# Attention in 32-column tiles, score groups of three PSUM banks, separate rings for weight pieces

## The chip, the cores and the metric

The kernel runs on one core of one Trainium2 chip. A core has a matrix engine (TensorE, PE in the profile, with its weight loads in a row of their own, PEld), a vector engine (DVE), a scalar engine (ACT), GpSimd (POOL, which here only starts DMAs) and a sync engine (SP, which only starts DMAs). Each engine works through its own list of instructions in order and waits on semaphores. The metric is the time of one execution on the device in microseconds (us); less is better.

## The reference

Attention with capped scores over 4 batches and 12 heads, 448 positions, head size 64, and then two layers that are alike: `relu(x @ w_in) ** 2 @ w_out`, for 1792 tokens, with 768 and 2048 columns.

```python
scores = scale * np.matmul(q, k.transpose(0, 1, 3, 2))
scores = cap * np.tanh(scores / cap)
scores = scores - np.max(scores, axis=-1, keepdims=True)
attn = np.exp(scores)
attn = attn / (np.sum(attn, axis=-1, keepdims=True) + 1e-09)
x = np.matmul(attn, v)            # then (tokens, 768)
h = np.maximum(x @ w_in, 0.0)
x = h * h @ w_out                 # and once more with other weights
```

The weights come as float64. The kernel takes their two words as integers and makes float32 of them.

## The kernel before

**Attention** goes over 24 pairs of heads, A and B, one pair a step (`PAIRS`). The keys of a pair make seven tiles of 128: three of A, three of B, and one tile R with the last 64 keys of both heads. Scores stand transposed, keys on partitions and the 448 queries along the row, so each score matmul is 128x448 in float32, which the trace shows as two MATMULs. In step n PE does, in this order (`attention`, the loop at the end): the scores of pair n, where A's matmul uses rows 0 to 63 of the array and B's rows 64 to 127, both at once (L321); the totals of pair n-1, a sum over keys by a matmul with 32 columns of ones, four at once into the four quarters of bank 7 (L367); the values of pair n-1, two matmuls of 64 columns at once into the halves of bank 6 (L353); the scores of tile R of pair n, over all 128 rows and columns (L321); the values of tile R of pair n-1, likewise (L349). ACT takes tanh in place and then exp out of PSUM (L334, L338), by groups of two tiles (`GROUPS`), with R alone; the groups of a pair take turns on three places of two banks each (ring `sc`: banks 0, 2, 4). DVE transposes the totals out of bank 7, adds quarters in four instructions, takes the reciprocal, transposes back (L376 to L388) and multiplies the values in bank 6 by it (L406).

**The layers** do each product in seven block products (a Strassen scheme, `NAMES`), each as three matmuls of split operands: high part of the weight by high and low part of x, low part of the weight by high part of x (L658 to L660), 4032 matmuls of 128x128 by 128x448 in all. Weights come in 224 pieces of six 128x128 blocks. A piece is loaded from DRAM by SP (`load` in `run_pass`, L623), ACT rounds its high part into a buffer `wh` (L591, 3 buffers), and DVE takes the difference (L186) into `wl`: before, that is the buffer in which the piece was loaded, so one ring of 6 buffers `wl` holds a piece from its load to PE's last use of it.

**Rounding of words.** `round_words` turns 68 units of float64 words into float32: SP loads a unit (`ww`, 2 buffers, L206), ACT scales the high words (L212), DVE does three bit operations (L215, L218, L221), POOL stores it. Each two units make a block, of which DVE also makes four sums (L244) that POOL stores; the buffers `wg` (4) are free after that. A unit must be stored before the weight pieces that read it are loaded.

**The order** of each engine's list comes from a planner (`Plan`): every operation has an engine, a cost, a place on a common scale (one unit is one weight piece, 18 matmuls; attention lies before 0, a step is `STEP` units), a due time that sorts the engine's candidates, and rings that it takes from and gives back to. The planner writes the lists; at run time each engine only follows its own. The due times of rounding come from a loop that spreads blocks over the scale by a rate (`room`, L749 to L757).

## Time and profile before

| what | us |
|---|---|
| median of 3 runs | 1054.51 (1054.08 to 1054.87) |
| the profiled execution: its own time | 1051.55 |
| the profiled execution: its span, first to last instruction | 1049.6 |
| PE busy | 1026.8 (98%) |
| DVE busy | 846.2 (81%) |
| ACT busy | 707.2 (67%) |
| PEld busy | 828.7 (79%) |
| POOL busy | 106.8 (10%) |

A busy share is a mean over the whole span. The program has two stages that differ: attention up to the first MATMUL of L658, and the layers. Rows of stretches (busy time in a stretch), of the chain that ended last, and of single instructions in order of time tell the stages apart.

### The profile page before, as it was taken

The page shows a single profiled execution, that of the slowest core. Times are in us where ns is not written, and L with a number is a line of the kernel's source. Part 1 is how long each engine was busy: PE and PEld are TensorE (multiplying, and loading weights), DVE is VectorE, ACT ScalarE, POOL GpSimd, SP SyncE. Part 2 cuts the span into 40 slices and gives each one's busy share as a digit, 9 for nine tenths or more (in the row PEclk, how much of TensorE's full clock was granted, in tenths as well). Part 3 has the DMA queues.
Part 4 walks back from the last instruction along what each step waited for, and adds up shares of the span by engine and source line. Part 5 has one row for each costly group of instructions (what it writes and reads, how often), then busy time and mean ns, then how long its engine had stood idle before and what let it go on. Part 6 is the DMA issues. An engine that isn't in the chain of part 4 may idle for free.

```text
span 1049.6 us, 15159 instructions
## 1 busy us (share of the span) xinstructions
PE 1026.8 (98%) x5088; PEld 828.7 (79%) x5088; DVE 846.2 (81%) x1252; ACT 707.2 (67%) x1011; POOL 106.8 (10%) x185
## 2 busy tenths in 40 slices
PE   7999999999999999999999999999999999999997
PEld 3333333499998899989898998898999999999996
DVE  3789887878899989888999999779996865589751
ACT  7999999777786664777865746778565444465641
POOL 0100121212111011011110121111000000000000
PEclk9999999999999999999999999999999999999999
DMA  8868899789878497679774976987556533334341
GB/s 208 277 208 253 266 288 329 256 292 294 278 240 278 136 330 249 224 264 317 253 236 138 341 264 197 299 287 249 175 153 218 157 112 107 105 111 124 113 146 53
DMA packets 106726, 231.53 MB, mean 221 GB/s; under 512 B 16336, under 2 KB 61648, under 8 KB 106640
## 3 DMA queue, kind: packets, MB, share of 16 engines
q1 hardware_dynamic: 91920, 171.88, 53.6%
q0 software_dynamic: 14720, 58.60, 14.6%
q8 instruction: 42, 0.69, 0.3%
q14 instruction: 44, 0.36, 0.1%
HBM read 166.33 MB, written 64.09 MB: 220 GB/s over the span
## 4 chain that ended last, share of the span: by engine, by line
PE 88%; DVE 5%; DMA 3%; issue 2%; ACT 1%; SPq 0%; POOL 0%; DVEq 0%; ACTq 0%; POOLq 0%
PE bank L660 23%; PE bank L659 23%; PE bank L658 23%; PE bank L321 8%; PE bank L353 6%; PE bank L367 4%; PE bank L349 2%; DMA ww<-wout_dram 2%; DVE wl L186 1%; DVE xc L186 1%; DVE wg L244 1%; DMA wl<-wo 1%; DVE wg L218 1%; DMA wo<-wg 1%; ACT p L338 0%
## 5 line engine op out<-in xcount | busy, mean ns | idle before, releaser
L660 PE MATMUL bank<-xc,wl 128*128 128x448 f32 x1344 | 492.8, 367 | 7.1 <-DVE wl L186 7.0
L658 PE MATMUL bank<-xc,wh 128*128 128x448 f32 x1344 | 492.4, 366 | 1.9 <-ACT xc L519 1.6
L659 PE MATMUL bank<-xc,wh 128*128 128x448 f32 x1344 | 492.1, 366 | 1.3 <-DVE xc L186 1.3
L591 ACT ACTIVATE wh<-wl 128x768 fp32r<-128x768 f32 x224 | 188.6, 843 | 198.9 <-PE bank L659 171.5
L186 DVE TENSOR_TENSOR wl<-wl,wh 128x768 fp32r<-128x768 f32 x224 | 211.5, 953 | 85.4 <-ACT wh L591 84.8
L660 PEld LDWEIGHTS bank<-xc,wl 128*128 128x128 f32 x1344 | 252.4, 188 | 32.0 <-DVE wl L186 10.4
L658 PEld LDWEIGHTS bank<-xc,wh 128*128 128x128 f32 x1344 | 252.5, 188 | 24.4 <-ACT xc L519 2.0
L659 PEld LDWEIGHTS bank<-xc,wh 128*128 128x128 f32 x1344 | 252.4, 188 | 23.8 <-DVE xc L186 1.9
L677 ACT ACTIVATE one<-bank 128x448 f32<-128x448 f32 x132 | 71.1, 539 | 66.5 <-PE bank L660 61.8
L321 PE MATMUL bank<-raw 64*128 64x448 f32 (+1 forms) x336 | 88.6, 575 | 6.2 <-DMA raw<-qk_dram 4.8
L334 ACT ACTIVATE bank<-bank,caps 128x896 f32<-128x896 f32 x96 | 84.5, 880 | 8.7 <-PE bank L321 8.4
L338 ACT ACTIVATE p<-bank,caps 128x896 f32<-128x896 f32 x96 | 87.8, 914 | 3.1
L679 DVE TENSOR_TENSOR one<-bank,one 128x448 f32<-128x448 f32 x96 | 59.0, 620 | 28.9 <-PE bank L660 22.2
L321 PEld LDWEIGHTS bank<-raw 64*128 64x128 f32 (+1 forms) x336 | 34.7, 191 | 57.6 <-ACT bank L334 16.5
L218 DVE SCALAR_TENSOR_TENSOR wg<-ww,wg 128x768 uint32<-128x768 uint32 (+1 forms) x68 | 61.9, 910 | 2.0
L221 DVE SCALAR_TENSOR_TENSOR wg<-ww,wg 128x768 uint32<-128x768 uint32 (+1 forms) x68 | 61.7, 907 | 1.6
L212 ACT ACTIVATE wg<-ww 128x768 f32<-128x768 f32 (+1 forms) x68 | 57.8, 860 | 5.8 <-DMA ww<-wout_dram 3.6
L353 PE MATMUL bank<-p,vr 128*64 128x448 f32 x288 | 59.4, 548 | 0.0
L353 PEld LDWEIGHTS bank<-p,vr 128*64 128x64 f32 x288 | 18.5, 136 | 39.8 <-issue 29.6
L186 DVE TENSOR_TENSOR xc<-ga,xc 128x896 fp32r<-128x896 f32 (+1 forms) x50 | 45.1, 916 | 0.7 <-ACT xc L519 0.6
L215 DVE TENSOR_SCALAR wg<-wg 128x768 uint32<-128x768 uint32 (+1 forms) x68 | 36.0, 530 | 9.0 <-ACT wg L212 9.0
L367 PE MATMUL bank<-p,ones 128*32 128x448 f32 x384 | 41.1, 545 | 0.0
(80 smaller groups left out, 828.4 us busy)
## 6 DMA issues: line engine op xcount, KB each, us to landing
ww<-win_dram SPq DMA_DIRECT2D x32, 768.0 KB, 6.8
wl<-si SPq DMA_DIRECT2D x120, 192.0 KB, 3.9
wl<-wi SPq DMA_DIRECT2D x96, 192.0 KB, 3.7
ww<-wout_dram SPq DMA_DIRECT2D x24, 768.0 KB, 7.5
wi<-wg POOLq DMA_DIRECT2D x32, 384.0 KB, 6.3
si<-wg POOLq DMA_DIRECT2D x32, 384.0 KB, 4.9
wl<-so SPq DMA_DIRECT2D x32, 384.0 KB, 3.8
raw<-qk_dram SPq DMA_DIRECT2D x48, 240.0 KB, 5.1
```

Of the source, the lines that this page charges most:

```text
L186: nc.vector.tensor_tensor(out, a, b, op=ALU.subtract)
L218: nc.vector.scalar_tensor_tensor(m["fu"], m["t"][:, :n, 0], 29, m["fu"], op0=ALU.logical_shift_right, op1=ALU.bitwise_or)
L321: nc.tensor.matmul(s["s"][:, i, :S], lhsT=stk["t"][rows, S + 128 * t:S + 128 * t + 128], rhs=stk["t"][rows, :S], start=True, stop=True)
L334: nc.scalar.activation(s["s"], s["s"], AF.Tanh, scale=rcap)
L338: nc.scalar.activation(s["p"], s["s"], AF.Exp, scale=capt)
L353: nc.tensor.matmul(bank[64 * e:64 * e + 64, 6, :S], lhsT=vt["t"][:, w:w + 64], rhs=s["p"][:, e], start=gi == 0, stop=False, skip_group_che ...
L367: nc.tensor.matmul(bank[32 * z:32 * z + 32, 7, :S], lhsT=ones[:, one], rhs=p, start=half == 0, stop=half == 1)
L591: nc.scalar.activation(m["hi"], m["f"], AF.Copy)
L658: nc.tensor.matmul(a, lhsT=hi, rhs=x(0), start=first and z == 0, stop=False, skip_group_check=more)
L659: nc.tensor.matmul(a, lhsT=hi, rhs=x(1), start=False, stop=False, skip_group_check=more)
L660: nc.tensor.matmul(a, lhsT=lo, rhs=x(0), start=False, stop=final and z == len(xs) - 1, skip_group_check=more)
L677: nc.scalar.activation(m[g, i, n], a, AF.Copy)
```

## The change

In attention everything on PE but the scores of the tiles of A and B now uses tiles of 128 rows and 32 columns, four at once: the values of the first three tile pairs (rows in `PARTS` order: A, B, A, B, each half of 32), the values of R, and the scores of R. The order in a step is scores, totals, values, values of R, scores of R; the scores of R are now last and go to bank 7, which they share with the totals (ring `dn` now hands out bank 7, taken by R's scores, given back by R's exp, taken again by the totals, given back by DVE's first transpose). The score groups are A0 B0 A1, and B1 A2 B2, of three banks each (ring `sc`: 0 and 3), and R. DVE needs two additions of 64 rows where there were four of 32. Since the values stand in another order of rows, the first layer's word loads pick rows in that order: 16 of the 68 units are loaded by four DMAs of 32 rows where there was one.

Weight pieces are loaded into a ring `wf` of 3 buffers, and DVE writes the low part into another ring `wl` of 3; a buffer `wf` is free as soon as the low part is made. The place of the load is 4 units ahead of use where it was 6. Due times of DVE's normalisation are earlier by `URGENT`, and the rates that spread rounding are 1.5, 1.4 and 0.6 where they were 1.3, 1.5 and 0.6.

```diff
-GROUPS = [[("A", t), ("B", t)] for t in range(3)] + [[("R", 3)]]
+GROUPS = [[("A", 0), ("B", 0), ("A", 1)], [("B", 1), ("A", 2), ("B", 2)], [("R", 3)]]
+PARTS = [(slice(32 * r, 32 * r + 32), slice(32 * z, 32 * z + 32)) for z, r in enumerate((0, 2, 1, 3))]
-STEP = 2.27
+STEP = 2.14
+URGENT = 2.0
...
-    w_lo = [wp.tile([128, KC, 128], F32R, name=f"wl{i}") for i in range(6)]
+    w_f = [wp.tile([128, KC, 128], F32, name=f"wf{i}") for i in range(3)]
+    w_lo = [wp.tile([128, KC, 128], F32R, name=f"wl{i}") for i in range(3)]
...
-            nc.sync.dma_start(m["t"][:, :n].rearrange("p (h m) w -> p h (m w)", h=2), src)
+            to = m["t"][:, :n].rearrange("p (h m) w -> p h (m w)", h=2)
+            for rows, own in PARTS if l == g == 0 else [(slice(0, 128), slice(0, 128))]:
+                nc.sync.dma_start(to[own], src[rows])
...
+                    if t == 3:
+                        for z in range(4):
+                            w = S + 384 + 32 * z
+                            nc.tensor.matmul(groups_of[n][2]["s"][32 * z:32 * z + 32, 0], lhsT=stk["t"][:, w:w + 32], rhs=stk["t"][:, :S],
+                                             start=True, stop=True)
+                        continue
...
-                if gi == 3:
-                    nc.tensor.matmul(bank[:, 6, :S], lhsT=vt["t"][:, 576:VL], rhs=s["p"][:, 0], start=False, stop=True, skip_group_check=True)
-                    return
-                for e in range(2):
-                    w = 192 * gi + 128 * e
-                    nc.tensor.matmul(bank[64 * e:64 * e + 64, 6, :S], lhsT=vt["t"][:, w:w + 64], rhs=s["p"][:, e],
-                                     start=gi == 0, stop=False, skip_group_check=True)
+                for z in range(4):
+                    e, h = z % 2, z // 2
+                    w = 192 * t + 128 * e + 32 * h if t < 3 else 576 + 64 * e + 32 * h
+                    nc.tensor.matmul(bank[32 * z:32 * z + 32, 6, :S], lhsT=vt["t"][:, w:w + 32], rhs=weights(n, t, e), start=t == 0, stop=t == 3)
...
-                for z in range(4):
-                    own, other = slice(32 * z, 32 * z + 32), slice(32 * (z ^ 1), 32 * (z ^ 1) + 32)
+                for z in range(2):
+                    own, other = slice(64 * z, 64 * z + 64), slice(64 - 64 * z, 128 - 64 * z)
...
-                totals(n - 1, 0, t + 0.66, 800)
-                r = inverse(n - 1, totals(n - 1, 1, t + 0.88, 800))
-                for gi in range(3):
-                    values(n - 1, gi, t + 1.1 + 0.2 * gi, 790)
+                totals(n - 1, 0, t + 0.64, 860)
+                r = inverse(n - 1, totals(n - 1, 1, t + 0.85, 750))
+                for k in range(3):
+                    values(n - 1, k, t + 1.05 + 0.2 * k, 750)
+                divide(n - 1, r, values(n - 1, 3, t + 1.66, 750))
             if n < len(PAIRS):
-                scores(n, (3,), t + 1.7, 850, drop=["raw"])
-            if n:
-                divide(n - 1, r, values(n - 1, 3, t + 1.9, 780))
+                scores(n, (3,), t + 1.87, 750, (2,), drop=["raw"])
...
-        w_part[s] = m, op("DVE", dve(KC * 128), lo, s - 1.9, [o])
+        w_part[s] = m, op("DVE", dve(KC * 128), lo, s - 1.9, [o], take=[("wl", m["wl"])], drop=[("wf", m["wf"])])
...
-            o = op("SP", (6 * 128 * 512, len(runs)), load, base + q - 6, deps, take=[("wl", m["wl"])])
+            o = op("SP", (6 * 128 * 512, len(runs)), load, base + q - 4, deps, take=[("wf", m["wf"])])
...
-                room += 0.5 * (1.3 if at_place < 0 else 1.5 if at_place % 56 < 28 else 0.6)
+                room += 0.5 * (1.5 if at_place < 0 else 1.4 if at_place % 56 < 28 else 0.6)
...
-        plan.emit({"ww0": 1, "ww1": 1, "wg": 4, "wh": 3, "wl": 6, "sc": [0, 2, 4], "pv": 1, "p": 7, "pr": 2,
-                   "raw": 3, "vr": 3, "d": 1, "y": 2, "dn": 1, "rn": 2, "o": 3, "m0": 1, "m1": 1,
+        plan.emit({"ww0": 1, "ww1": 1, "wg": 4, "wf": 3, "wh": 3, "wl": 3, "sc": [0, 3], "pv": 1, "p3": 4, "p1": 2,
+                   "raw": 3, "vr": 3, "d": 1, "y": 2, "dn": [7], "rn": 2, "o": 3, "m0": 1, "m1": 1,
```

What this does to the lists of the engines, at three places. Lines are those of the kernel before and of the changed one (+15 or so further down).

PE, one step of attention (`raw` queries and keys, `p` the exponentials, `vr` the values), before:

```order
L321 MATMUL bank<-raw 128x448 x6
L367 MATMUL bank<-p,ones 32x448 x8
L353 MATMUL bank<-p,vr 64x448 x6
L321 MATMUL bank<-raw 128x448
L349 MATMUL bank<-p,vr 128x448
```

Such a step now, with buffer numbers (the three `p` of one pair are its three groups):

```order
L336 MATMUL bank_206<-raw_269 128x448 x6
L382 MATMUL bank_206<-p_323,ones_254 32x448 x3
L382 MATMUL bank_206<-p_346,ones_254 32x448 x3
L382 MATMUL bank_206<-p_367,ones_254 32x448 x2
L372 MATMUL bank_206<-p_323,vr_246 32x448 x5
L372 MATMUL bank_206<-p_346,vr_246 32x448
L372 MATMUL bank_206<-p_323,vr_246 32x448
L372 MATMUL bank_206<-p_346,vr_246 32x448 x5
L372 MATMUL bank_206<-p_367,vr_246 32x448 x4
L330 MATMUL bank_206<-raw_269 32x448 x4
```

Between the six score matmuls and the next six, three kinds of tile (32, 64 and 128 columns) have become one kind of 32 columns, with R's scores at the end.

ACT, the end of attention (the last pair's tanh and exp, `wh` a weight piece's high part, `wg` words), before:

```order
L591 ACTIVATE wh2_238<-wl2_241 128x768
L334 ACTIVATE bank_206<-bank_206,caps_174 128x2x448
L338 ACTIVATE p_1681<-bank_206,caps_174 128x896
L334 ACTIVATE bank_206<-bank_206,caps_174 128x2x448
L338 ACTIVATE p_1696<-bank_206,caps_174 128x896
L334 ACTIVATE bank_206<-bank_206,caps_174 128x2x448
L338 ACTIVATE p_1704<-bank_206,caps_174 128x896
L334 ACTIVATE bank_206<-bank_206,caps_174 128x448
L338 ACTIVATE p_1714<-bank_206,caps_174 128x448
L212 ACTIVATE wg2_232<-ww0_234 128x768
```

And now:

```order
L217 ACTIVATE wg2_232<-ww0_234 128x768
L348 ACTIVATE bank_206<-bank_206,caps_174 128x3x448
L352 ACTIVATE p_1890<-bank_206,caps_174 128x1344
L348 ACTIVATE bank_206<-bank_206,caps_174 128x3x448
L217 ACTIVATE wg3_233<-ww1_235 128x768
L352 ACTIVATE p_1922<-bank_206,caps_174 128x1344
L348 ACTIVATE bank_206<-bank_206,caps_174 128x448
L352 ACTIVATE p_1930<-bank_206,caps_174 128x448
L217 ACTIVATE wg0_230<-ww0_234 128x512
```

Two units of words that stood behind the last exp (the second not shown) now stand ahead of it, inside the last pair's groups.

DVE, in the first layer's second product, the last unit of that layer's words (`wg1`, 128x512) and the low part of the weight piece behind it, before, where that is piece 31 of the 224 (counted from 0):

```order
L215 TENSOR_SCALAR wg1_231<-wg1_231 128x512
L244 TENSOR_TENSOR wg0_230<-wg0_230 128x384
L244 TENSOR_TENSOR wg0_230<-wg2_232,wg0_230 128x384
L244 TENSOR_TENSOR wg2_232<-wg0_230,wg2_232 128x384
L244 TENSOR_TENSOR wg2_232<-wg2_232 128x384
L218 SCALAR_TENSOR_TENSOR wg1_231<-ww1_235,wg1_231 128x512
L221 SCALAR_TENSOR_TENSOR wg1_231<-ww1_235,wg1_231 128x512
L679 TENSOR_TENSOR one_2586<-bank_206,one_2586 128x448
L186 TENSOR_TENSOR wl1_240<-wl1_240,wh1_237 128x768
```

And now, where it is piece 28:

```order
L189 TENSOR_TENSOR xc9_216<-ga_1982,xc2_209 128x896
L189 TENSOR_TENSOR ga_1982<-gb_1983,ga_1982 128x896
L220 TENSOR_SCALAR wg1_231<-wg1_231 128x512
L223 SCALAR_TENSOR_TENSOR wg1_231<-ww1_235,wg1_231 128x512
L226 SCALAR_TENSOR_TENSOR wg1_231<-ww1_235,wg1_231 128x512
L189 TENSOR_TENSOR wl1_243<-wf1_240,wh1_237 128x768
```

That unit of words now comes three weight pieces earlier, and the four sums of another block no longer stand inside it.

## Rows read from the trace of the kernel before

**Rows 1.** Busy time by stretch: us, engines' busy us (instructions), clock, DMA share, GB/s.

```profile
22.00:202.00 180.00, 180.00 (x968) 64.15 (x964) 148.45 (x304) 172.83 (x211) 24.86 (x44) 1.00 0.87 273
210.00:1040.00 830.00, 819.68 (x4004) 750.69 (x4003) 685.69 (x921) 515.82 (x777) 77.66 (x124) 1.00 0.65 212
300.00:360.00 60.00, 55.77 (x270) 50.23 (x269) 59.18 (x72) 39.49 (x55) 8.00 (x12) 1.00 0.61 202
630.00:670.00 40.00, 37.19 (x180) 33.29 (x179) 35.28 (x56) 28.34 (x48) 6.24 (x9) 1.00 0.74 236
```

**Rows 2.** The chain that ended last, in order of time: start, us, what.

```profile
21.51 2.46 PE bank L321 x12
...
193.88 2.46 PE bank L321 x12
...
202.08 1.73 PE bank L367 x16
```

**Rows 3.** PE's weight loads in one step of attention: start, us, line, output<-input.

```profile
119.91 0.30 PEld L321 LDWEIGHTS bank<-raw 64*128 64x128 f32 x4 [0.65 <-ACT bank L334]
...
120.39 0.19 PEld L321 LDWEIGHTS bank<-raw 64*128 64x128 f32 x2 [0.18 <-issue]
...
121.52 0.19 PEld L321 LDWEIGHTS bank<-raw 64*128 64x128 f32 x2 [0.18 <-issue]
...
122.36 0.16 PEld L367 LDWEIGHTS bank<-p,ones 128*32 128x32 f32 x8 [0.65 <-DVE xc L186]
...
122.77 0.13 PEld L367 LDWEIGHTS bank<-p,ones 128*32 128x32 f32 x4 [0.25 <-issue]
...
124.00 0.20 PEld L353 LDWEIGHTS bank<-p,vr 128*64 128x64 f32 x4 [0.73 <-issue]
...
126.41 0.30 PEld L321 LDWEIGHTS bank<-raw 128*128 128x128 f32 x2 [0.70 <-ACT p L338]
...
128.11 0.30 PEld L321 LDWEIGHTS bank<-raw 64*128 64x128 f32 x4 [0.65 <-ACT xc L458]
```

**Rows 4.** Groups by line and form, 0 to 255 us: busy us, mean ns | idle before.

```profile
L338 ACT ACTIVATE p<-bank,caps 128x896 f32<-128x896 f32 x72 | 72.6, 1008 | 2.4
...
L212 ACT ACTIVATE wg<-ww 128x768 f32<-128x768 f32 x24 | 21.5, 906 | 1.2 <-DMA ww<-wout_dram 1.2
...
L338 ACT ACTIVATE p<-bank,caps 128x448 f32<-128x448 f32 x24 | 15.2, 634 | 0.8
...
L458 ACT ACTIVATE xc<-m 128x448 fp32r<-128x448 f32 x15 | 8.1, 567 | 0.0
```

**Rows 5.** ACT in that step, two groups of two tiles: start, us, line.

```profile
122.73 1.01 ACT L338 ACTIVATE p<-bank,caps 128x896 f32<-128x896 f32 x1
...
123.63 0.97 ACT L334 ACTIVATE bank<-bank,caps 128x896 f32<-128x896 f32 x1
...
124.64 1.01 ACT L338 ACTIVATE p<-bank,caps 128x896 f32<-128x896 f32 x1
```

**Rows 6.** Instructions at attention's start: first tanh, first totals.

```profile
7.68 0.98 ACT L334 ACTIVATE bank<-bank,caps 128x896 f32<-128x896 f32 x1 [4.37 <-PE bank L321]
...
15.69 0.16 PEld L367 LDWEIGHTS bank<-p,ones 128*32 128x32 f32 x8 [0.65 <-issue]
```

**Rows 7.** Instructions at attention's end: last exp, first matmul of the layers.

```profile
202.17 0.64 ACT L338 ACTIVATE p<-bank,caps 128x448 f32<-128x448 f32 x1
...
206.65 0.71 PE L658 MATMUL bank<-xc,wh 128*128 128x448 f32 x1
```

**Rows 8.** PE's waits from 204 us: us in total, times, longest us.

```profile
PE bank L660 <- DVE wl L186: 7.0, 6, 2.0
```

**Rows 9.** DVE between two low parts of weight pieces, at 448 to 457 us.

```profile
449.19 0.55 DVE L215 TENSOR_SCALAR wg<-wg 128x768 uint32<-128x768 uint32 x1
...
456.23 0.95 DVE L186 TENSOR_TENSOR wl<-wl,wh 128x768 fp32r<-128x768 f32 x1
```

More of the change, by code (lines that the diff above doesn't have):

```diff
@@ L359, in totals @@
         def totals(n, half, place, cost):
-            s = groups_of[n]
             def emit():
-                for e in range(2):
-                    for gi in (2 * half, 2 * half + 1):
-                        z = 2 * e + gi % 2
-                        one, p = (1 + e, s[gi]["p"][:, 0]) if gi == 3 else (0, s[gi]["p"][:, e])
-                        nc.tensor.matmul(bank[32 * z:32 * z + 32, 7, :S], lhsT=ones[:, one], rhs=p, start=half == 0, stop=half == 1)
-            return pe(cost, emit, place, [s[gi]["done"] for gi in (2 * half, 2 * half + 1)], take=[] if half else ["dn"])
+                for t in (2 * half, 2 * half + 1):
+                    for e in range(2):
+                        z = 2 * (t % 2) + e
+                        nc.tensor.matmul(bank[32 * z:32 * z + 32, 7, :S], lhsT=ones[:, 1 + e if t == 3 else 0], rhs=weights(n, t, e),
+                                         start=half == 0, stop=half == 1)
@@ L371, in inverse @@
+            return pe(cost, emit, place, ready(n, 2 * half, 2 * half + 1), take=[] if half else ["dn"])
         def inverse(n, done):
```

68 lines of the change are left out of this document (39 added, 29 removed).

## The prediction

> **What bounds the kernel now.** I read the busy shares in the table first: PE at 98%, all others lower. Busy time by stretch then splits that [rows 1]. Between 22 and 202 us, in attention, PE is busy all of the time, and ACT is nearly so: 172.8 of 180 us. Between 210 and 1040 us, in the layers, PE is busy 819.7 of 830 us, so it stands idle for 10.3 us, 4.2 of them between 300 and 360 us and 2.8 between 630 and 670 us; in the former DVE is busy 59.2 of 60 us. The granted clock is 1.00 in all these stretches, the level of 2.4 GHz. The chain that ended last confirms it: it runs through PE, step after step [rows 2]. The scores of pair 2 start at 21.51 us and those of pair 23 at 193.88 us, 21 steps of 8.21 us.
>
> What is in such a step is to be seen in the weight loads [rows 3]. Sections start at 119.91 (scores), 122.36 (totals), 124.00 (values), 126.41 (128 columns, R) and again at 128.11 us: 2.45, 1.64, 2.41 and 1.70 us. Inside a section the loads follow each other every (121.52 - 120.39) / 3 = 0.377 us, which is one half of a float32 matmul; I call it a slot. Scores have 6 slots (2.26 us), totals 4 (1.51), values 6 (2.26), the last section 4 (1.51). So each entry into a section costs 0.19, 0.13, 0.15 and 0.19 us, 0.66 us a step: the first load of a new tile shape waits until the array is empty (0.65 to 0.73 us of idle loader ahead of it, against 0.18 to 0.25 inside a section), and the matmul waits for the load.
>
> **The change part by part, PE in attention.** The new list has the same 20 slots: 6 of scores, then 4 of totals, 8 of values (three tile pairs and R), 2 of R's scores, all 14 in tiles of 32 columns. It has two entries instead of four. Scores stay at 2.45 us; the long section takes 14 x 0.377 + 0.13 = 5.41 us, its entry being that of the totals, the same shape. A step is 7.86 us, 0.34 less. That the four quarters of a value slot run at once I take from the totals, which do it with four different inputs. From the scores of pair 2 to the totals of the last pair there are 22 steps: **-7.5 us**.
>
> Row against rule: the loads of the totals' second slots begin at 122.77 us, take 0.13 us and don't stretch the slots [rows 3]. The Trainium skill, "TensorE: Matmul & The Clock Gate", Part 3 on row and column tiling, says that a weight load overlaps running matmuls only where its row group differs from theirs, and here all 32-column tiles use all rows; by that rule each of the 14 slots would also pay its load. The trace speaks against it, so it has a small place among the rivals.
>
> **Start.** The first tanh is at 7.68 us and the first totals at 15.69 us [rows 6]; in between ACT does the groups of pair 0. A group of two tiles takes 1.01 us (tanh to exp) plus 0.90 us (exp to the next tanh) [rows 5], 1.92 us. From 448 to 896 elements exp grows by (1008 - 634) / 448 = 0.83 ns each [rows 4], so the new group of 1344 takes 1.92 + 2 x 0.37 = 2.66 us, and R at most 2 x 0.634 = 1.27 us. The first new group needs a third tile, some 0.7 us later than 7.68 (two slots at about half speed). Then 8.4 + 2 x 2.66 + 1.27 = 15.0 us, when bank 7 is free and the totals can go, against 15.69; with the wait for the scores of pair 1 I take **-0.3 us** (0 to -0.6).
>
> **End.** Before, the last exp (202.17, 0.64 us) ran beside the last totals, which began at 202.08 and lost 0.1 us, and the layers began at 206.65 [rows 2, 7]. Now R's scores are the last thing before the totals, these need bank 7, which R's exp gives back, and no scores of a next pair lie between. That costs at least 1.27 us. The order also puts two scalings of words (0.91 us each [rows 4]) among the last pair's groups: counted from the start of that step, ACT is free at 1.2, then 0.91 + 2.66 + 2.66 + 0.91 + 1.27 gives 9.6 us, and PE would be ready at 7.9. I take **+1.8 us** (1.3 to 2.5). The totals and values that follow take the same 12 slots and 0.13 us as they did (4.65 us against 206.65 - 202.08 = 4.57, counted from just behind the first load).
>
> **ACT in attention** must keep up: 2 x 2.66 + 1.27 = 6.6 us a step for tanh and exp, and the order gives it 20 scalings of words, 15 splits of x and 3 of weights there, (23 x 0.906 + 15 x 0.567) / 24 = 1.2 us a step [rows 4]. That is 7.8 us against PE's 7.86. It looks too close, but the same sum for before is 3 x 1.92 + 1.27 + (21 x 0.906 + 15 x 0.567) / 24 = 8.2 us against 8.20, and there PE kept its step. What is new is how early PE needs ACT. R's exp must be over when the totals begin, 2.45 us after R's scores end; 1.27 is needed, so one scaling fits in between and two don't. The second group must be out of its banks when the second score tile of the next pair begins, 0.85 us into the step. Going through the 24 steps of ACT's list by these durations, its lateness stays under those limits, with two scalings in a step followed by a step with none. I cost it at **0** (up to +5 us if the words' loads come late, since all later groups are queued behind such a wait on ACT, and PE behind them).
>
> **Costed at nothing:** DVE does half as many additions, and it was idle 31.5 of 180 us in attention. Its first transposition must now end before R's scores, 8 slots or 3.0 us after the totals, where it had a step; the due times put it ahead, and one operation of rounding in its way fits. The 48 more DMA issues of SP (16 units in four parts) stand ahead of loads of queries and values that have three buffers and are wanted two steps later. If that cover were gone, PE would wait from the first score on.
>
> **The layers.** Matmuls are unchanged. Idle time comes from DVE's list: PE waits for the low part `wl`, 7.0 us in 6 waits, at most 2.0 [rows 8], as where DVE works through rounding from 449.19 to 456.23 us between two low parts [rows 9]; three pieces ahead (18 matmuls or 819.7 / 4004 x 18 = 3.7 us each) is all that the ring of `wh` allows, less the two roundings of a piece, so a lump beyond some 9 us stalls PE. Rounding comes earlier now: about one and a half units more are done when the layers begin, and in the middle of the first layer the last units stand three pieces earlier and no longer in one lump with sums. So I let the 4.2 us between 300 and 360 us go. The other 6.1 us I let stand: the lump of rows 9 is gone, but before the pieces 48 and 60 stand new ones that are longer (nine and fourteen instructions, among the latter two whole units of words), and at 630 to 670 us the list is much as it was. The new rings change little: `wl` with 3 buffers waits for PE as `wh` does anyway, and a load can start when the low part three pieces before is made, some 2 us later than it could. **-4 us** (-8 to +3: nearly all idle time gone, or two waits of 2.0 and one more added and nothing won).
>
> **Sum:** -7.5 - 0.3 + 1.8 + 0 - 4 = -10.0 us. On the profiled execution the span goes from 1049.6 to 1039.6 and its time from 1051.55 to 1041.6. The median of the runs lies 3.0 us above that execution's time; the same difference from it gives **1044.5 us**.
>
> **The rivals.**
> - Better: the end costs nothing and all but 2 us of the layers' idle time goes: -7.8 - 8 = -15.8, 1038.7 us. For it: less rounding in the busiest stretch. Against: the lumps at 48 and 60. Chance 0.07.
> - ACT sets attention's pace. Words that land late, or two scalings ahead of R's exp, and the step stays near 8.1 us: 22 x 0.1 = 2.2 instead of 7.5, so -2.2 - 0.3 + 1.8 - 4 = -4.7, 1049.8 us. For it: 7.8 of 7.86 us, and DMA at 0.87 before [rows 1] with more bytes in less time. Against: no such wait before at the same load. Chance 0.14.
> - Slower: weight pieces come late. With three buffers `wf`, a load waits for DVE, and SP's list is in order: a load that waits holds the words behind it, these hold ACT's scaling, and that holds DVE. Each late piece costs what the two places at 300 to 360 us cost, 2.1 us. From the third on (6.0 / 2.1) attention's gain is eaten; seven, with no gain in the layers, give 7 x 2.1 - 6.0 = +8.7, 1063.2 us. For it: DVE runs at 83% in the layers. Against: before, low parts were made no earlier either. Chance 0.08.
> - It doesn't do what it says: value quarters run two at a time. Eight more slots, 24 x 3.0 = 72 us: 1117 us. By the rule of the Trainium skill on loads, of the same page, it would be 14 x 0.13 x 24 = 44 us more, 1088 us. Chance of either 0.03.
>
> **How the numbers follow.** My forecast has 0.68. Its own spread is about 1041 to 1048. For 8 in 10 the range takes in the third rival and most of the first: 1039 to 1051. A measurement of this kernel tells 0.2%, 2.1 us, from no change. Faster: 0.68 + 0.07 and most of ACT's case, 0.09, makes 0.84; the rest of it, where the layers win nothing too, is the same, 0.05; slower is 0.08 + 0.03 = 0.11.
>
> **What would show it.** Score sections 7.86 us apart in the chain, two long idle loaders a step instead of four, and four value loads in each slot 0.377 us apart. ACT's groups at 2.66 us. A wait of PE for the last exp of about 1.8 us, and the layers' first matmul near 200.6 us. PE idle some 6 us between there and the end, little of it in the second product of the first layer. I am wrong on PE if the long section takes over 5.6 us; on ACT if PE waits for exp or for scores' banks in mid attention; on the layers if waits for `wl` come in places where no lump of rounding stands.

## The result, and the profile after

The changed kernel takes 1045.56 us (median of 4 runs, 1043.62 to 1047.15) against 1054.69 us (4 runs, 1054.08 to 1056.63) of the kernel before in the same comparison: a ratio of 0.9915, 95% interval 0.990 to 0.993. That is faster by 9.1 us; the forecast was 1044.5 us, 10.0 less. The profiled execution took 1043.62 us with a span of 1041.9 us, 7.7 us less span than before.

The weight loads of PE in one step of attention of the changed kernel (start, us, line, output<-input, and in brackets the loader's idle time and what ended it), to be read against [rows 3]:

```profile
121.16 0.13 PEld L372 LDWEIGHTS bank<-p,vr 128*32 128x32 f32 x4 [0.24 <-issue]
121.54 0.13 PEld L330 LDWEIGHTS bank<-raw 128*32 128x32 f32 x4 [0.25 <-issue]
...
122.78 0.30 PEld L336 LDWEIGHTS bank<-raw 64*128 64x128 f32 x4 [0.73 <-issue]
...
125.23 0.16 PEld L382 LDWEIGHTS bank<-p,ones 128*32 128x32 f32 x8 [0.65 <-ACT p L352]
...
126.01 0.13 PEld L382 LDWEIGHTS bank<-p,ones 128*32 128x32 f32 x4 [0.25 <-issue]
126.39 0.13 PEld L372 LDWEIGHTS bank<-p,vr 128*32 128x32 f32 x4 [0.25 <-issue]
```

The loader idles long (0.73 and 0.65 us) at the scores of 64 rows and at the totals alone. From totals to values (126.01 to 126.39) and from values to R's scores (121.16 to 121.54) it goes on at 0.375 us a slot, as if nothing had changed, and four value loads lie in each slot.

The end of attention on PE (a timeline: start, us, line, count, and the wait ahead):

```profile
185.62 2.53 PE L336 MATMUL bank<-raw 64*128 64x448 f32 x12
...
192.71 0.96 PE L330 MATMUL bank<-raw 128*32 128x448 f32 x8
195.50 1.71 PE L382 MATMUL bank<-p,ones 128*32 128x448 f32 x16 [1.83 <-ACT p L352]
198.03 3.21 PE L372 MATMUL bank<-p,vr 128*32 128x448 f32 x32 [0.82 <-DVE o L422]
201.18 0.47 PE L674 MATMUL bank<-xc,wh 128*128 128x448 f32 x1
```

The scores of the last pair in the kernel before, in the same view:

```profile
193.81 2.53 PE L321 MATMUL bank<-raw 64*128 64x448 f32 x12
```

Two waits stand one behind the other: the last totals for R's exp, and the values for DVE's division of the pair before (L422), which gives back bank 6. The layers begin at 201.18 us against 206.65 [rows 7]. ACT, and below it DVE, there:

```profile
190.81 1.35 ACT L348 ACTIVATE bank<-bank,caps 128x1344 f32<-128x1344 f32 x1
192.07 0.94 ACT L217 ACTIVATE wg<-ww 128x768 f32<-128x768 f32 x1
192.90 1.38 ACT L352 ACTIVATE p<-bank,caps 128x1344 f32<-128x1344 f32 x1
...
194.81 0.64 ACT L352 ACTIVATE p<-bank,caps 128x448 f32<-128x448 f32 x1
```

```profile
193.50 0.65 DVE L404 STREAM_TRANSPOSE rn<-dq 128x448 f32<-128x448 f32 x1
194.07 0.92 DVE L226 SCALAR_TENSOR_TENSOR wg<-ww,wg 128x768 uint32<-128x768 uint32 x1
...
196.48 0.96 DVE L226 SCALAR_TENSOR_TENSOR wg<-ww,wg 128x768 uint32<-128x768 uint32 x1
197.36 0.62 DVE L422 TENSOR_TENSOR o<-bank,rn 128x448 f32<-128x448 f32 x1
```

A scaling of words stands between tanh and exp of the last pair, and four operations of rounding stand ahead of the division, which could have run at 194.1 us.

Busy time by stretch of the changed kernel (columns as in [rows 1]; the second stretch is the layers from their first matmul to the last):

```profile
22.00:195.00 173.00, 171.67 (x1492) 60.50 (x1488) 141.37 (x266) 166.55 (x170) 25.96 (x46) 1.00 0.96 285
201.18:1035.60 834.42, 826.40 (x4036) 757.76 (x4032) 682.87 (x914) 515.77 (x777) 77.20 (x123) 1.00 0.65 210
300.00:360.00 60.00, 60.00 (x296) 55.24 (x295) 57.73 (x67) 37.85 (x53) 5.54 (x9) 1.00 0.66 203
630.00:670.00 40.00, 39.70 (x195) 36.23 (x194) 32.32 (x49) 29.88 (x51) 6.24 (x9) 1.00 0.83 286
720.00:724.00 4.00, 1.94 (x8) 1.77 (x9) 4.00 (x6) 1.99 (x3) 0.68 (x1) 0.89 0.56 113
724.00:728.00 4.00, 4.00 (x16) 3.62 (x15) 3.93 (x6) 2.06 (x3) 0.00 (x0) 0.68 1.03 361
```

In the layers PE idles 834.42 - 826.40 = 8.0 us; before it was 10.3 us [rows 1]. Nothing of it lies between 300 and 360 us now, and 0.3 us between 630 and 670 us. PE's waits from 204 us on, to be read against [rows 8]:

```profile
PE bank L676 <- DVE wl L189: 6.8, 6, 2.4
PE bank L674 <- ACT one L693: 1.2, 1, 1.2
```

By the starts of the matmuls the long pauses stand at 279.79 us (1.58 us from one start to the next, where 0.20 is usual), 380.62 (1.39), 427.08 (2.50) and 722.07 (2.76). Behind the last of them the granted clock falls: 0.89 and 0.68 in the two windows above, and nine matmuls follow each other every 0.373 us instead of 0.204, so they run at 1.2 GHz instead of 2.4. Summed over both windows that is (1 - 0.89) x 4 + (1 - 0.68) x 4 = 1.7 us. The kernel before had no such stretch in its profile ahead of its last matmul.

### The profile page after: what moved, and what is told of

It is laid out like the page before. It is cut to its first block, busy times and chain, and to the rows that moved or that the text cites. A ratio compares the mean times of both kernels' runs of the same rounds, so it can differ in the third digit from the quotient of the medians.

```text
span 1041.9 us, 16113 instructions
## 1 busy us (share of the span) xinstructions
PE 1019.5 (98%) x5664; PEld 826.9 (79%) x5664; DVE 834.3 (80%) x1204; ACT 698.8 (67%) x963; POOL 106.6 (10%) x185
## 4 chain that ended last, share of the span: by engine, by line
PE 91%; DVE 3%; DMA 2%; ACT 1%; issue 1%; SPq 0%; DVEq 0%; ACTq 0%
PE bank L676 25%; PE bank L674 25%; PE bank L675 25%; PE bank L372 6%; PE bank L336 5%; PE bank L382 3%; PE bank L330 1%; DMA wf<-si 1%; DMA ww<-wout_dram 1%; DVE wl L189 1%; DVE xc L189 1%; ACT bank L348 1%; ACT p L352 0%; DVE wg L223 0%; DMA raw<-qk_dram 0%
## 5 line engine op out<-in xcount | busy, mean ns | idle before, releaser
L607 ACT ACTIVATE wh<-wf 128x768 fp32r<-128x768 f32 x224 | 187.8, 842 | 175.0 <-PE bank L675 146.0
L189 DVE TENSOR_TENSOR wl<-wf,wh 128x768 fp32r<-128x768 f32 x224 | 212.0, 953 | 80.6 <-ACT wh L607 79.7
L348 ACT ACTIVATE bank<-bank,caps 128x1344 f32<-128x1344 f32 (+1 forms) x72 | 79.3, 1102 | 9.1 <-PE bank L336 7.0
L352 ACT ACTIVATE p<-bank,caps 128x1344 f32<-128x1344 f32 (+1 forms) x72 | 81.6, 1133 | 2.2
L372 PE MATMUL bank<-p,vr 128*32 128x448 f32 x768 | 76.6, 539 | 0.8 <-DVE o L422 0.8
L336 PE MATMUL bank<-raw 64*128 64x448 f32 x288 | 64.7, 570 | 5.4 <-DMA raw<-qk_dram 4.7
L372 PEld LDWEIGHTS bank<-p,vr 128*32 128x32 f32 x768 | 24.9, 110 | 48.3 <-issue 44.0
L336 PEld LDWEIGHTS bank<-raw 64*128 64x128 f32 x288 | 28.3, 192 | 41.0 <-issue 22.3
```

The costliest lines, as they stand in the source:

```text
L189: nc.vector.tensor_tensor(out, a, b, op=ALU.subtract)
L336: nc.tensor.matmul(groups_of[n][gi]["s"][:, at], lhsT=stk["t"][rows, S + 128 * t:S + 128 * t + 128], rhs=stk["t"][rows, :S], start=True, s ...
L348: nc.scalar.activation(s["s"], s["s"], AF.Tanh, scale=rcap)
L352: nc.scalar.activation(s["p"], s["s"], AF.Exp, scale=capt)
L372: nc.tensor.matmul(bank[32 * z:32 * z + 32, 6, :S], lhsT=vt["t"][:, w:w + 32], rhs=weights(n, t, e), start=t == 0, stop=t == 3)
L607: nc.scalar.activation(m["hi"], m["f"], AF.Copy)
```

## The experiments

The runs were made in three sets, each on one chip and beside the kernel before (medians 1053.46, 1053.24 and 1052.75 us). So they are compared by their ratio to it; the last column is the distance from the changed kernel, (ratio - 0.9915) x 1053 us. With the width of the intervals, about 1.5 us each way, distances under 2 to 3 us say little by themselves, and there the traces decide.

| run | median us | ratio (95%) | layers begin, us | PE idle in layers, us | against the changed kernel, us |
|---|---|---|---|---|---|
| changed kernel | 1045.56 | 0.9915 (0.990 to 0.993) | 201.18 | 8.0 | |
| R as one matmul | 1049.44 | 0.9961 (0.9948 to 0.9975) | 206.53 | 7.7 | +4.8 |
| values of 64 columns | 1051.78 | 0.9983 (0.9971 to 0.9994) | 207.17 | 8.2 | +7.2 |
| score groups of two | 1051.67 | 0.9977 (0.9964 to 0.9989) | 206.27 | 8.1 | +6.5 |
| old rates | 1055.94 | 1.0028 (1.0017 to 1.0040) | 199.68 | 17.6 | +11.9 |
| old rates, ring of six | 1053.72 | 1.0010 (0.9999 to 1.0021) | 199.94 | 16.3 | +10.0 |
| ring of six | 1041.65 | 0.9888 (0.9870 to 0.9905) | 199.49 | 9.2 | -2.8 |
| rings of three, earlier loads | 1047.93 | 0.9954 (0.9937 to 0.9970) | 204.68 | 7.2 | +4.1 |
| last pair's banks | 1048.21 | 0.9949 (0.9935 to 0.9964) | 205.09 | 7.7 | +3.6 |
| later due times | 1048.17 | 0.9949 (0.9934 to 0.9964) | 200.88 | 10.8 | +3.6 |
| both of these | 1050.74 | 0.9975 (0.9966 to 0.9984) | 198.77 | 14.6 | +6.3 |
| ring of six, last pair's banks | 1041.90 | 0.9902 (0.9886 to 0.9919) | 199.44 | 8.6 | -1.4 |
| the same, rate 1.6 | 1044.17 | 0.9917 (0.9900 to 0.9934) | 202.59 | 6.8 | +0.2 |

### Is it the entries? R as one matmul, values of 64 columns

Theory: the step is shorter because there are fewer new tile shapes. Rival: the order and the larger groups of ACT did it.

```diff
-                        for z in range(4):
-                            w = S + 384 + 32 * z
-                            nc.tensor.matmul(groups_of[n][2]["s"][32 * z:32 * z + 32, 0], lhsT=stk["t"][:, w:w + 32], ...
+                        nc.tensor.matmul(groups_of[n][2]["s"][:, 0], lhsT=stk["t"][:, S + 384:S + 512], ...
```

> Base is the changed kernel, R's scores alone are again one matmul of 128 columns on 128 rows, in the same place (same 2 slots of 0.377 us). Theory 1, a new tile shape costs its entry: one entry more a step, 0.15 us as in the kernel before, so score sections 8.01 us apart instead of 7.86, three long idle loaders a step, and 23 x 0.15 = +3.4 us in the span. Theory 2, the gain came from the new order and ACT's larger groups and not from the shapes: steps stay at 7.86 us, 0.0 us.

The chain of the run with R as one matmul (start, us, what), and its weight loads at that matmul:

```profile
20.95 2.46 PE bank L333 x12
29.00 2.46 PE bank L333 x12
```

```profile
124.61 0.30 PEld L328 LDWEIGHTS bank<-raw 128*128 128x128 f32 x2 [0.73 <-DVE wg L220]
125.56 0.30 PEld L333 LDWEIGHTS bank<-raw 64*128 64x128 f32 x4 [0.65 <-ACT p L349]
```

Steps are 8.05 us, 0.20 longer (expected 0.15), and a third long idle loader stands there. 22 steps make 4.4 us. The layers begin 5.4 us later; a fall of the clock at 200 us, worth 1.7 us, is in that too (last section).

```diff
-                for z in range(4):
-                    e, h = z % 2, z // 2
-                    w = 192 * t + 128 * e + 32 * h if t < 3 else 576 + 64 * e + 32 * h
-                    nc.tensor.matmul(bank[32 * z:32 * z + 32, 6, :S], lhsT=vt["t"][:, w:w + 32], ...
+                for e in range(2):
+                    w = 192 * t + 128 * e if t < 3 else 576 + 64 * e
+                    nc.tensor.matmul(bank[64 * e:64 * e + 64, 6, :S], lhsT=vt["t"][:, w:w + 64], ...
```

> Base is the changed kernel, the values alone are again in tiles of 64 columns (two matmuls a slot instead of four), R's part too; the halves of the result stand in the order A, B again. Theory 1 (entries cost): two entries more a step, 0.15 us into the values and 0.13 us into R's scores, so steps of 8.14 us and 23 x 0.28 = +6.4 us. Theory 2 (order and groups): 0.0 us. If four matmuls of 32 columns cost more than two of 64, the sections of values become shorter than 8 x 0.377 = 3.0 us here.

The chain of the run with values of 64 columns (start, us, what):

```profile
21.12 2.46 PE bank L336 x12
29.26 2.46 PE bank L336 x12
```

8.14 us a step, as worked out; the layers begin 6.0 us later, and the time is +7.2 us against +6.4. Value slots are 0.375 us there too, so four matmuls of 32 columns cost what two of 64 do. The rival falls: both runs keep the groups of three, the rates and the order, and lose the step.

### Are the larger groups needed? Score groups of two banks

```diff
-GROUPS = [[("A", 0), ("B", 0), ("A", 1)], [("B", 1), ("A", 2), ("B", 2)], [("R", 3)]]
+GROUPS = [[("A", t), ("B", t)] for t in range(3)] + [[("R", 3)]]
...
-        plan.emit({..., "sc": [0, 3], "pv": 1, "p3": 4, "p1": 2,
+        plan.emit({..., "sc": [0, 2, 4], "pv": 1, "p2": 7, "p1": 2,
```

> Base is the changed kernel, scores again in groups of two banks (three of them and R) for tanh and exp; PE's list of shapes is the new one, R stays in bank 7. Theory 1, the shorter step needs the larger groups, as ACT would set the pace without them: ACT's work is 3 x 1.92 + 1.27 + 1.2 = 8.2 us a step by the pairs of instructions (7.9 by its busy time before), so steps of 8.0 to 8.2 us, PE waits for exp or for banks in mid attention, +3 to +7.5 us. Rival: the groups are not needed, ACT has enough slack between its instructions: steps stay at 7.86, +0 to +1 us.

PE's waits in mid attention (timeline of PE, rows with a wait for ACT):

```profile
69.73 1.02 PE L336 MATMUL bank<-raw 64*128 64x448 f32 x4 [0.50 <-ACT p L351]
104.10 1.71 PE L380 MATMUL bank<-p,ones 128*32 128x448 f32 x16 [1.72 <-ACT p L351]
143.89 1.02 PE L336 MATMUL bank<-raw 64*128 64x448 f32 x4 [1.08 <-ACT p L351]
```

The kernel is 6.5 us slower, as expected in size. But the picture of an even step of 8.0 to 8.2 us was wrong: most steps keep 7.86 us (20.40, 28.25, 36.11 us in the chain), and the debt is paid in three waits, 3.3 us, and at the end, so that the layers begin 5.1 us later (1.7 us of this is a fall of the granted clock behind the wait there, of which more below). ACT's busy time from 22 to 195 us is 168.9 us against 166.6. The groups were needed: without them attention loses 5.1 of the 5.5 us that it had won.

### What did the new rates do? Old rates, with rings of three and with a ring of six

```diff
-                room += 0.5 * (1.5 if at_place < 0 else 1.4 if at_place % 56 < 28 else 0.6)
+                room += 0.5 * (1.3 if at_place < 0 else 1.5 if at_place % 56 < 28 else 0.6)
```

> Base is the changed kernel, the rounding of words is spread by the old rates (1.3, 1.5 and 0.6 instead of 1.5, 1.4 and 0.6). Theory 1, the layers' idle time follows DVE's lumps of rounding: less is done in attention, PE's idle time between 300 and 360 us comes back (over 3 us there, waits for the low part), that behind pieces 48 and 60 (380 and 427 us) goes, in sum +1 to +6 us; attention stays at 7.86 us a step. Rival, the rings made the difference in the layers: 300 to 360 us stays without idle time, 0 to -1 us.

Busy time by stretch with the old rates, the whole of the layers and 300 to 360 us:

```profile
199.68:1046.80 847.12, 829.54 (x4036) 758.52 (x4032) 688.65 (x921) 516.59 (x778) 79.91 (x127) 0.99 0.64 209
300.00:360.00 60.00, 52.82 (x249) 47.39 (x248) 57.50 (x69) 35.13 (x49) 6.60 (x10) 0.94 0.65 208
```

The place is as expected and the size was far off: +11.9 us, not +1 to +6. Attention is even 1.5 us shorter, but PE idles 17.6 us in the layers, 7.2 of them at 300 to 360 us, and is busy 3.1 us longer there at a mean clock of 0.99. The longest wait there is 5.17 us: PE stands behind ACT's `wh`, ACT behind DVE's addition for `one`, and DVE was in a lump of rounding from 316.75 to 320.65 us. With these rates the changed kernel is slower than the kernel before, by 0.28%. What was open was whether the rings of three share in this:

> Base is the run with the ring of six (1041.65 us), with the old rates of rounding (1.3, 1.5, 0.6). Theory 1, the old rates cost because attention is 6 us shorter and so leaves more rounding to the layers, whatever the rings: idle time in the layers rises by 6 us or more as it did with rings of three (+8.4), total near 1049 to 1052 us. Rival, the old rates cost only together with the rings of three: the layers stay as before the change (836 us from first to last matmul), total within 3 us of 1041.65.

They don't. With the ring of six the old rates cost 12.8 us by the ratios (1.0010 against 0.9888), somewhat more than expected, and PE idles 16.3 us in the layers, 7.1 more. The longest wait stands in the second layer this time; ahead of it DVE was in a lump of rounding from 738.20 to 742.10 us:

```profile
199.94:1045.75 845.81, 829.55 (x4036) 759.26 (x4032) 687.99 (x920) 516.31 (x778) 79.39 (x126) 0.99 0.64 209
```

```profile
745.71 0.74 PE L673 MATMUL bank<-xc,wh 128*128 128x448 f32 x1 [7.29 <-ACT wh L606]
```

The kernel before had the same rates and idled 10.3 us. The rates count in places, one piece of weights of the layers each, and attention is 24.7 x 2.14 = 52.9 places now instead of 24.7 x 2.27 = 56.1, so that at an unchanged rate the due times of later blocks fall later in the layers. Less rounding done in attention is not what the traces show: of the 68 scalings of words 20 start before the layers with the old rates, with either ring, as in the kernel before, and 21 in the changed kernel. What moves is the rest. The last scaling of the first layer's words starts 116 us behind the layers' first matmul with the old rates (114 with the ring of six), 111 us in the kernel before and 100 us in the changed kernel. That the old rates cost is shown. That these later lumps are the cause is argued: the edit changes the rate in attention and the rate in the layers at once, no run changed one alone, and the pause at 745 us lies far from attention.

### What did the rings do? Ring of six, and rings of three with earlier loads

```diff
-    w_f = [... range(3)]
-    w_lo = [... range(3)]
+    w_lo = [... range(6)]
...
-                m["f"] = w_f[m["wf"][0]]
+                m["lo"] = w_lo[m["wl"][0]]
+                m["f"] = m["lo"].bitcast(F32)
...
-            o = op("SP", ..., load, base + q - 4, deps, take=[("wf", m["wf"])])
+            o = op("SP", ..., load, base + q - 6, deps, take=[("wl", m["wl"])])
```

> Base is the changed kernel, weight pieces again in one ring of six, the low part written over the loaded piece, loads placed two pieces earlier. Theory 1, rings of three change little, as the ring of the high parts holds PE three pieces ahead anyway: within 1.5 us of the changed kernel, PE idle 8 +- 2 us in the layers, attention the same. Rival, the separate rings bring part of the layers' gain: idle time in the layers at 11 us or more, waits for DMA on ACT's or DVE's side, +3 us.

1041.65 us, and the four runs lie within 0.8 us. PE idles 9.2 us in the layers, so the rings of three gave no clear gain there. I expected attention to stay as it was and the time to stay within 1.5 us; attention ends 1.7 us earlier, and the time is 2.8 us less. The end on PE with the ring of six:

```profile
192.51 0.94 PE L329 MATMUL bank<-raw 128*32 128x448 f32 x8
194.85 1.71 PE L381 MATMUL bank<-p,ones 128*32 128x448 f32 x16 [1.40 <-ACT p L351]
...
199.49 0.47 PE L673 MATMUL bank<-xc,wh 128*128 128x448 f32 x1
```

No wait for the division is left, and the exp is done 0.65 us earlier: in this order one scaling of words stands in the last step ahead of R's exp (191.26 us), in the changed kernel two (187.37 and 192.07). Either the earlier loads or the depth of the ring could be behind that.

```diff
-            o = op("SP", ..., load, base + q - 4, deps, take=[("wf", m["wf"])])
+            o = op("SP", ..., load, base + q - 6, deps, take=[("wf", m["wf"])])
```

> Base is the changed kernel, its two rings of three kept, only the loads of weight pieces placed two pieces earlier, as the kernel before and the run with the ring of six had them. Theory 1, the ring of six won 1.7 us at the end of attention because its first pieces were issued earlier (ACT's scheduled rounding of the third piece stood in front of the softmax and waited for that load: 0.19 us in the changed kernel, 1.4 to 1.9 us in the runs on the end): here ACT doesn't wait for that piece either and the layers begin near 199.5 us, the total like the ring of six, some 2 us under the changed kernel. Rival, depth of the ring (six pieces of loads in flight, in-place low parts): layers begin near 201.2 us as in the changed kernel, 0 us.

Neither theory gave the number. ACT doesn't wait for that load, as the first said, yet the layers begin at 204.68 us: two scalings stand inside the last pair again, the totals wait 2.02 us and the values 1.97, and the clock is low from the first wait until behind the second (32 value matmuls take 5.00 us instead of 3.2, and the window below is at 0.57):

```profile
195.54 2.24 PE L382 MATMUL bank<-p,ones 128*32 128x448 f32 x16 [2.02 <-ACT p L352]
199.75 5.00 PE L372 MATMUL bank<-p,vr 128*32 128x448 f32 x32 [1.97 <-DVE o L422]
```

```profile
200.00:204.00 4.00, 4.00 (x28) 1.03 (x24) 1.62 (x5) 0.67 (x1) 0.68 (x2) 0.57 0.89 290
```

So earlier loads alone don't bring what the ring of six brings. What differs at the end of attention is where the planner's order happens to put scalings and rounding: between the last pair's reciprocal, transposed back (`rn`), and the division that waits for it stand three operations of rounding with the ring of six, four in the changed kernel and ten here. That the depth of the ring is worth something beyond this isn't shown.

### What bounds the end? Other banks for the last pair, later due times, both

```diff
-            o = pe(cost, emit, place, ..., take=[("sc" if gi < 2 else "dn", groups_of[n][gi]["at"]) for gi in taken], **more)
+            o = pe(cost, emit, place, ..., take=[("sc" if gi < 2 or n == len(PAIRS) - 1 else "dn", groups_of[n][gi]["at"]) for gi in taken], **more)
...
-                r = inverse(n - 1, totals(n - 1, 1, t + 0.85, 750))
+                if n < len(PAIRS):
+                    r = inverse(n - 1, totals(n - 1, 1, t + 0.85, 750))
                 for k in range(3):
                     values(n - 1, k, t + 1.05 + 0.2 * k, 750)
+                if n == len(PAIRS):
+                    r = inverse(n - 1, totals(n - 1, 1, t + 1.55, 750))
```

> Base is the changed kernel; for the last pair alone R's scores go to a bank of the first group, and the totals of the first half and the values of three tile pairs go ahead of the totals of the second half, so that neither bank 7 nor R's exp is waited for. Theory 1 (what bounds the end is DVE's division of pair 22, which gives back bank 6 behind rounding and is over at 197.98 us): PE's waits for bank 7 (0.5) and for R's exp (1.8) go, but the values still start at 198.0 us and now have the second totals behind them, so the layers begin at 198.0 + 3.2 + 0.75 = 202.0 us against 201.18, +0.8 us. Rival (R's exp bounds the end): the layers begin 1.5 to 2 us earlier, near 199.4 us.

PE's waits from 185 to 205 us:

```profile
PE bank L372 <- DVE o L422: 2.7, 1, 2.7
PE bank L382 <- ACT p L352: 1.8, 2, 1.1
```

The wait for the division, 2.7 us, took the place of most of the others, which is theory 1, with the sign right; but 0.8 us became 3.9 (205.09 us). 1.1 us of it, PE's first wait for exp, came from a wait of ACT for the load of a weight piece, 1.94 us at 187 us (0.19 in the changed kernel), though the order up to there is the same, and a fall of the clock behind the wait adds 1.7 us.

```diff
+            due += 2.6 if -6 < due < -3 else 1.4 if -3 < due < 0 else 0
             round_block(l, g, i, k, due - 8, 2.4, due)
```

> Base is the changed kernel; only the due times of the two blocks of words at the end of attention are set later (by 2.6 and 1.4 places), so that DVE's divisions stand ahead of the rounding and one scaling less stands ahead of the last exp on ACT. Theory 1: the last exp ends some 0.6 us earlier (194.85 instead of 195.45), the values don't wait for DVE (0.82), so the layers begin near 199.75 us, 1.4 us earlier; in the layers the two blocks cost nothing or give part back: -1.4 us, or 0 if given back. Rival (DVE's order doesn't bound the end): layers begin at 201.2 us, 0 us.

The division isn't waited for any more. The exp still is, 1.8 us, ACT having again waited 1.53 us for that load, and the layers begin at 200.88 us (199.75 expected). In the layers the two blocks come back: PE idles 10.8 us, with a new pause at 249 us (3.13 us from start to start), and the kernel is 3.6 us slower.

With both edits in one kernel:

> Base is the changed kernel with both edits, the last pair's banks and order and the later due times. Theory 1 (two waits in turn, each hides the other): R's scores start near 192.2 us, the first totals near 193.3, the values without a wait at 194.8, the layers near 198.6 us, 2.6 us earlier than 201.18, so -2.6 us, more than the sum of the two alone (+0.8 - 1.4). Rival (something third holds the end, as the first weight pieces or the first split x): the layers begin no earlier than with the later due times alone.

The end went as theory 1 had it: from R's scores on PE's timeline with both edits shows no wait, and the layers begin at 198.77 us (expected 198.6).

```profile
193.36 0.93 PE L330 MATMUL bank<-raw 128*32 128x448 f32 x8
...
194.86 2.48 PE L372 MATMUL bank<-p,vr 128*32 128x448 f32 x24
```

2.4 us are won there and 6.6 us of idle time are lost in the layers, all of it now waits for the low part:

```profile
PE bank L679 <- DVE wl L189: 14.6, 10, 4.1
```

I had expected the two blocks to cost nothing there. With the ring of six, where the division comes early without later due times, and the edit to the last pair's banks:

> Base is the run with the ring of six, with the other banks and order for the last pair. There R's exp held the first totals 1.40 us and DVE's division of pair 22 was over at 195.33 us, so by theory 1 (two waits in turn) the first totals start at 193.5 us, the values at 195.3, and the layers at 195.3 + 3.2 + 0.75 = 199.2 us against 199.49: -0.3 us, since the division takes the place of the exp. Rival (the exp alone bounds): the layers begin 1.4 us earlier, 198.1 us.

The exp's wait went and the division's came, 0.91 us, so the layers begin at 199.44 us, 0.05 us earlier; the time is that of the ring of six.

```profile
193.45 1.20 PE L381 MATMUL bank<-p,ones 128*32 128x448 f32 x8
195.55 2.46 PE L371 MATMUL bank<-p,vr 128*32 128x448 f32 x24 [0.91 <-DVE o L421]
```

And with more rounding in attention:

```diff
-                room += 0.5 * (1.5 if at_place < 0 else ...
+                room += 0.5 * (1.6 if at_place < 0 else ...
```

> As the run with the ring of six and the last pair's banks, with more rounding in attention (rate 1.6 instead of 1.5). Theory 1: no scaling stands between the last pair's groups and the division comes right behind its reciprocal, so the layers begin near 198.4 us (-1.1 against 199.49), and DVE's lumps in the layers shrink (waits for the low part from 8.5 us to about 6): some -3 us against the ring of six, 1038.6 us, no long gap and so no fall of the granted clock. Rival: ACT has no room for 1.3 scalings more in attention, PE waits for exp in mid attention, +1 to +3 us there, total 1041 to 1043 us.

The rival was nearer: PE waits in attention, and 1044.17 us lies above even its 1041 to 1043. Its reason isn't shown. Ahead of PE's wait for exp stands a wait of ACT for words (second fence), and the other waits in attention are for DVE's first transposition (`tn`). The third fence is from the layers:

```profile
PE bank L381 <- ACT p L351: 1.5, 1, 1.5
PE bank L329 <- DVE tn L391: 1.3, 2, 0.8
```

```profile
182.63 0.89 ACT L216 ACTIVATE wg<-ww 128x768 f32<-128x768 f32 x1 [1.19 <-DMA ww<-wout_dram]
```

```profile
PE bank L678 <- DVE wl L188: 3.0, 3, 2.0
```

The waits for the low part shrink from 8.4 to 3.0 us, so the rounding did move, but the layers begin 3.15 us later. Of the rates in attention that ran, 1.3 (with 1.5 in the layers), 1.5 and 1.6, the middle one is the best.

The best version is the changed kernel with the ring of six: 0.9888 of the kernel before (0.9870 to 0.9905), below the changed kernel's 0.9915 (0.990 to 0.993). The intervals overlap a little, so that it beats the changed kernel is likely and not certain.

## Why the prediction was right, and where it wasn't

That the median came out within 1.1 us is partly luck. The profiled execution took 1043.62 us where 1041.6 was forecast, and the median lies 1.9 us above it, not 3.0; and the terms are off both ways.

**PE's step** held: 7.86 us was forecast, and the scores of pair 2 start at 20.66 us and those of pair 23, 21 steps on, at 185.62 us, so 7.855. 22 steps give 22 x (8.208 - 7.855) = 7.8 us instead of 7.5. The sum left out a 23rd, since its start ends at the first totals and its steps begin at the scores of pair 2: 8.1 us in all. The two runs on shapes price the entries apart, 0.20 us for R's 128 columns and 0.28 for the pair that 64 columns bring. The Trainium skill ("TensorEngine Tiling (Array Packing)", Key Properties) says that changing the tiling mode drains the engine; the idle loaders agree, and these are its prices here. The rule of the Trainium skill on loads that the prediction weighed and set aside ("TensorE: Matmul & The Clock Gate", Part 3) doesn't hold in this trace: 0.375 us a slot with a load of 0.13 us behind a load of the same rows.

**The start** gave -0.43 us against -0.3 (first totals at 15.26 us).

**The end** was mis-sized. From the scores of the last pair to the layers it takes 201.18 - 185.62 = 15.6 us, 12.8 before (206.65 - 193.81), so 2.7 us more, although the step inside that stretch is 0.35 us shorter: the end costs 3.1 us against the 1.8 forecast. The wait for R's exp is 1.83 us, as forecast. The step that failed is that the totals and values behind it take the same time as they did: the division that frees bank 6 stood behind four operations of rounding. "Costed at nothing" named DVE's first transposition and not the division at the other end of the same chain. Attention in all gave -0.43 - 8.1 + 3.1, or -5.5 us, forecast -6.0.

**ACT at nothing** held: no wait in mid attention. That this was close, as the sum of 7.8 us said, is borne out from two sides: smaller groups bring waits of 3.3 us, and rate 1.6 brings 1.5 us for ACT, which waited for words, and 1.3 us for DVE's first transposition, which "Costed at nothing" names.

**The layers** were mis-sized: -2.3 us against -4. Two things that I read from the order came true: the 4.2 us between 300 and 360 us went, and the lumps before pieces 48 and 60 stall PE (1.39 and 2.50 us). A third did not: the 2.8 us between 630 and 670 us, which I let stand, went too, all but 0.3. In their place came what I hadn't seen: ACT's wait for words, 2.41 us before 278.42, behind which `one` and then PE stood, and the wait at 722 us with the fall of the clock. There DVE does three operations of rounding and three others between the low parts at 714.73 and 721.06 us, a lump of 5.5 us, where I had taken some 9 us as the limit.

The base of that term was wrong, and the total doesn't show it. I let the new rates win against the kernel before. But against the new, shorter attention with the old rates they win 9.6 us of idle time, and without them the change is no gain at all. Rounding does come earlier, as I said, though by one scaling when the layers begin and not one and a half. The step that failed is that PE's shorter steps were booked whole: at the old rates PE idles 17.6 us in the layers instead of 10.3, a cost which the sum put at nothing on one side and hid in the gain of the rates on the other. What attention won there, 7.0 us, the layers took back and more. Why they do stays open as far as said above.

**The rings** I took at "little". In the layers that is so (9.2 against 8.0 us of idle time). In all, the ring of six came out 2.8 us faster, in its profile by 1.7 us at the end of attention and by no fall of the clock. That the rings as such are behind this isn't shown.

**The rivals.** That pieces come late stayed small in the profiled run of the changed kernel (ACT waits 0.19 us at 185.5) and was there in four others (1.0 us with R as one matmul, 1.4 to 1.9 us in the runs on the end), as a wait in ACT's list ahead of the softmax; the rival priced it, at 2.1 us a piece, by two places in the layers. The quarters of the values don't run two at a time: four loads lie in each slot.

## What to carry to other kernels

When work is hidden beside a stage, plan it anew when that stage becomes shorter, before the gain is booked: left at its old rates it cost more in the next stage here than the shorter steps had won. Count changes of tile shape in the loop, not matmuls; each cost 0.14 to 0.20 us here. At the end of a software pipeline go through every buffer that the last stage takes back and through the queue of the engine that frees it: here each wait found hid the next, and what was pushed out came back in the layers at more than its price (2.4 us won, 6.6 lost).

## What the hardware showed that I had not expected

Pauses of PE cost more than their length, in some executions. At a pause the granted clock was seen to fall to 1.2 GHz for a stretch, which cost 1.7 us in most cases and 3.4 us in three (at 197 us with earlier loads, 321 us with the old rates, 744 us with the old rates and the ring of six). In the profiles such falls stand at pauses (from matmul start to matmul start) of 2.76 us at 722 us in the changed kernel; of 2.26, 2.50 and 2.80 us in the run with R as one matmul; of 2.75, 2.50 and 2.75 in that with groups of two; of 3.28, 2.50 and 2.76 in that with the last pair's banks; of 2.76 with values of 64 columns, 2.29 at 746 us with the old rates, 2.34 at 643 us with rate 1.6, and some more in the rest. The first of each three stands at the end of attention, the others in the layers. The same pause of 2.50 us at 427 to 433 us, behind the lump before piece 60, was followed by a fall in three profiles and by none in five, that of the changed kernel among them (first row). Shorter pauses do not rule it out: with rate 1.6 a fall stands behind two pauses of 1.94 and 1.15 us at 341.58 and 342.73 us (second row), while the kernel before had two of 1.93 and 1.15 us, at 347.40 and 348.55 us, and no fall:

```profile
428.00:432.00 4.00, 4.00 (x21) 3.69 (x20) 3.97 (x6) 1.96 (x3) 0.08 (x1) 1.00 1.03 383
```

```profile
344.00:348.00 4.00, 4.00 (x15) 3.60 (x14) 3.69 (x4) 1.43 (x4) 0.00 (x0) 0.66 0.00 0
```

The kernel before had pauses up to 2.35 us and no fall in its profile ahead of its last matmul; but its executions beside the other runs have mean granted clocks from 0.995 to 0.999, where the profiled one has 0.999, so some of them probably had falls too. The two kernels with the ring of six and the rate 1.5, whose longest pauses in the layers are 1.94 and 1.93 us, had none in their profiles and a mean granted clock of 0.998 to 1.000 in all ten runs (1041.22 to 1041.99 us in four runs of the first, 1041.34 to 1043.74 us in six of the second). The changed kernel's four runs have 0.996 to 0.998 and lie 3.5 us apart; but the slowest of them is one with 0.998, so the falls alone don't order them, and what makes up the rest of that spread stays open.
